# A chunked recurrence feeding a feed-forward layer on one Trainium2 core: the scores of unit 13 and two row splits are planned two steps later

## The chip, the cores and the metric

One NeuronCore of a Trainium2 chip runs the whole program. The metric is the device time of one execution in microseconds (us), median of the runs. The profile is one execution, taken by the hardware profiler. It shows five engines: PE (matmul; PEld is its weight load), DVE (VectorE), ACT (ScalarE), POOL (GpSimd) and SP, which here only issues DMAs. An engine works through its own instructions strictly in the order in which they stand in its program, and waits for semaphores of the others.

## The reference, cut to what is computed

A recurrence over 768 tokens per batch and head (4 batches, 8 heads, head size 32, state size 16), in chunks of 32 tokens, and then a feed-forward layer over all 3072 tokens (256 to 2048 to 256):

```
for c in range(S // 32):                       # chunk c of 32 tokens
    L = exp(cum_i - cum_j) * causal            # decays within the chunk
    y[c] = ((C @ B.T) * L) @ x + (C @ state) * exp(cum)
    state = decay_full * state + sum_j B_j x_j * decay_from_j
x = y as [3072, 256]
h = x @ w_in                                   # 256 -> 2048
g = softplus(h)
out = g @ w_out                                # 2048 -> 256
```

## The kernel before, in words

**Units and tiles.** The recurrence is cut into 24 units (`NB * NU`) of 128 tokens, six to a batch, with all heads in one unit. The feed-forward layer works on six tiles (`sizes`) of 512 tokens, so four units fill one tile: units 8 to 11 are the third tile (index 2), units 12 to 15 the fourth (index 3). The first 12 units are worked off in a hand-written order (`ORDER`, lines 59 to 76), and so is much of tiles 0 and 1. From unit 12 on (`FIRST`) the units are planned into steps (lines 919 to 926).

**Steps.** A step `s` stands for one tile and one block `k` of 128 of the 2048 hidden columns (line 896). Its first product, `hp`, is six matmuls of 512 columns on PE; then ACT makes `e` (softplus) and `gh` (the rounded high part), and DVE makes `gl` (the remainder). Four steps later (`LAG`) the second product takes `gh` and `gl` and adds six matmuls into two accumulators, `acc0` and `acc1`. There is one PSUM buffer for each of the two accumulators (pool `pa`, line 116). When a tile, or a half of the tiles 0 and 1, ends, DVE reads both out (`o0`, `o1`, line 803, which for tile 1 also adds the half kept in `half_1`) before PE may start the next tile's sums in them. Steps 0 to 31 are tiles 0 and 1, step 32 is the third tile's block 0, and its second product is therefore called at step 36. At such a step the next first product is put ahead of it (lines 937 and 938), so that two first products, twelve matmuls, stand on PE between the last sum of tile 1 and the first of the third tile.

**A unit's work, in the order in which it is planned.** `prefetch` loads the unit's rows (`un`, 256 KB), its spread B and C rows (`bc`, 512 KB) and, for each pair, the growth factors (`gg`). `split_whole` makes `c_all` (odd units) or `kc` (even units) from `bc` on ACT and DVE, has it copied by two DMAs into `c_rows`, of which there is a single buffer, and makes `b_rows`. `attend_scores` has POOL make the masked decays `rm`, PE the scores `sp` from `c_rows` and `b_rows`, and DVE the weighted scores `m`, then `bp` and `cc`. `pair_values` and `pair_ends` follow for a pair of units: `zp` and `yp` on PE, `state` and `tb` on DVE, then the output `y` and its parts `xh` and `xl`, which are the tile's input to the first products.

**What sets the order.** PE's instructions and SP's DMAs stay in the order in which the code calls them (lines 133 and 137 to 139). Up to step 30 (`PINNED`) the order on ACT, DVE and POOL is the code's as well; what is called from step 31 on is put in place there by the framework's scheduler, which may set it among the earlier, fixed instructions. All DMAs go through SP's queue: one that waits holds back all behind it.

**Names.** In profile rows buffer numbers are left out. In the order's rows `m13_1624` is the weighted scores of unit 13, `gl2_3` is block 3 of the third tile, `o0_1` is the half 0 of the output of tile 1, and the number at the end only tells buffers apart. A row of the order that has several equal instructions says so (x2).

Of the kernel before, what the change touches and what calls it, by code (L numbers as in the profile page):

```python
# [76 lines left out]
HALF = NFT // 2  # L77
AHEAD = 28
PINNED = 31
LAG = 4  # L80
# [26 lines left out]
def recurrence_then_ffn(ctx: ExitStack, tc: tile.TileContext, fst, un, alr, w_in, w_out, const, outT):  # L107
# [801 lines left out]
    def plan(s, f, *args):  # L909
        fills[s].append((f, args))  # L910

    def through(f):
        def run(*args):
            for _ in f(*args):
                pass

        return run

    for i in range(FIRST, NB * NU):
        s = 30 + 4 * (i - FIRST)  # L920
        plan(max(s - 4, AHEAD), split_whole, i)
        plan(s, attend_scores, i)
        plan(s + 1, prefetch, i + 3)
        if i % 2:
            plan(s + 2, through(pair_values), i - 1)
            plan(s + 3, through(pair_ends), i - 1)
# [73 lines left out]
```

## Time and profile before

| | us |
|---|---|
| median of 3 runs (325.82 to 326.68) | 326.49 |
| the profiled execution | 326.83 |
| its span, first to last instruction | 325.1 |
| PE busy (1974 instructions) | 318.3 (98%) |
| DVE busy | 190.6 (59% of the span) |
| ACT busy | 191.1 (59%) |
| POOL busy | 39.4 (12%) |

In the views below, times count from the span's start. A timeline row has the start, the duration, the engine, the line, the operation with its tiles, and in brackets how long the engine sat idle before it and which instruction released it. SPq rows are DMA issues: the time shown is what SP took to hand the transfer over, not the transfer. A matmul of 512 columns is shown with 0.39, but the next one starts about 0.23 after it; starts are what to compare. The line of most instructions is that of a helper (L129), so the tiles tell them apart. A row of the view by stretches has the stretch, then the busy time of PE, PEld, DVE, ACT and POOL with the instructions in brackets, the granted clock, the DMA engines' busy share and GB/s.

### The profile page before, as it was taken

How to read it: one execution, taken by the hardware profiler on the slowest of the kernel's cores; microseconds unless marked ns; L12 is line 12 of the kernel's file. 1: busy time of each engine (PE TensorE's matmuls, PEld its weight loads, DVE VectorE, ACT ScalarE, POOL GpSimd, SP SyncE). 2: the span in 40 equal slices, each digit the busy share in tenths (PEclk: the TensorE clock that was granted, in tenths of full speed). 3: DMA queues.
4: the chain of work that ended last, by engine and by line, in shares of the span. 5: the costliest groups of instructions: out<-in, count | busy, mean ns of one | idle time of the engine just before them, and what ended most of it. 6: DMA issues, size and time to landing. Idle time of an engine off the chain costs nothing.

```text
span 325.1 us, 5266 instructions
## 1 busy us (share of the span) xinstructions
PE 318.3 (98%) x1974; PEld 255.7 (79%) x1974; DVE 190.6 (59%) x338; ACT 191.1 (59%) x349; POOL 39.4 (12%) x42
## 2 busy tenths in 40 slices
PE   8999999999999999899999999999999999999996
PEld 3568888888878888588888888888888888888885
DVE  3799767889584566775646746675744433322222
ACT  4898989797877565544433824644633344544450
POOL 3545300210300001102202101012100000000000
PEclk9999999999999999999999999999999999999999
DMA  6949658661732154335125246125201000100001
GB/s 222 394 152 359 212 187 214 176 194 46 246 100 66 65 151 124 107 124 143 32 99 159 70 130 146 51 97 161 86 14 34 0 2 0 53 12 2 1 0 65
DMA packets 25178, 36.53 MB, mean 112 GB/s; under 512 B 2112, under 2 KB 13504, under 8 KB 25152
## 3 DMA queue, kind: packets, MB, share of 16 engines
q1 hardware_dynamic: 25152, 36.19, 36.0%
q8 instruction: 15, 0.25, 0.3%
q14 instruction: 11, 0.09, 0.1%
HBM read 28.74 MB, written 3.24 MB: 98 GB/s over the span
## 4 chain that ended last, share of the span: by engine, by line
PE 88%; DVE 4%; DMA 3%; SPq 2%; issue 2%; ACT 0%; POOL 0%; DVEq 0%; ACTq 0%; POOLq 0%
PE hp L129 38%; PE acc L129 37%; PE yp L129 6%; PE sp L129 4%; PE warm L129 2%; DMA un<-in_un 2%; SPq L139 2%; DMA bc<-in_un 1%; PE zp L129 1%; PE end L129 1%; DVE m L129 1%; DVE w L129 1%; PE gp L129 0%; DVE b_rows L292 0%; DVE o L803 0%
## 5 line engine op out<-in xcount | busy, mean ns | idle before, releaser
L732 DVE TENSOR_TENSOR gl<-e,gh 128x512 fp32r<-128x512 f32 x65 | 49.8, 771 | 50.0 <-ACT gh L726 48.9
L129 PE MATMUL hp<-xh,wih 128*128 128x512 f32 (+1 forms) x204 | 77.6, 380 | 0.0
L129 PE MATMUL hp<-xl,wih 128*128 128x512 f32 (+1 forms) x204 | 76.9, 377 | 0.0
L129 PE MATMUL hp<-xh,wil 128*128 128x512 f32 (+1 forms) x204 | 76.8, 377 | 0.0
L720 ACT ACTIVATE e<-hp 128x512 f32<-128x512 f32 x65 | 38.7, 595 | 64.6 <-PE hp L129 64.2
L129 PE MATMUL acc<-gh,woh 128*128 128x512 f32 x188 | 74.9, 399 | 1.5 <-DVE o L803 1.5
L129 PE MATMUL acc<-gh,wol 128*128 128x512 f32 x188 | 73.4, 390 | 0.1
L129 PE MATMUL acc<-gl,woh 128*128 128x512 f32 x188 | 73.5, 391 | 0.0
L129 PEld LDWEIGHTS hp<-xh,wih 128*128 128x128 f32 x204 | 38.4, 188 | 8.3 <-DVE xl L129 1.0
L726 ACT CAST gh<-e 128x512 fp32r<-128x512 f32 x65 | 40.2, 619 | 6.7 <-PE acc L129 4.0
L129 PEld LDWEIGHTS hp<-xh,wil 128*128 128x128 f32 x204 | 38.3, 188 | 7.1
L129 PEld LDWEIGHTS hp<-xl,wih 128*128 128x128 f32 x204 | 38.4, 188 | 6.9
L129 PEld LDWEIGHTS acc<-gh,woh 128*128 128x128 f32 x188 | 35.4, 188 | 9.0 <-DVE o L803 1.4
L129 PEld LDWEIGHTS acc<-gh,wol 128*128 128x128 f32 x188 | 35.3, 188 | 8.1 <-DVE wol L129 0.6
L129 PEld LDWEIGHTS acc<-gl,woh 128*128 128x128 f32 x188 | 35.4, 188 | 6.4 <-DVE gl L732 0.2
L402 POOL TENSOR_SCALAR_AFFINE_SELECT rm<-fc 128x1024 f32<-128x1024 f32 x11 | 16.8, 1531 | 129.8 <-DVE m L457 97.2
L129 DVE TENSOR_TENSOR gl<-e,gh 128x512 fp32r<-128x512 f32 x31 | 21.5, 701 | 9.6 <-ACT gh L129 9.5
L129 POOL TENSOR_SCALAR_AFFINE_SELECT rm<-fc 128x1024 f32<-128x1024 f32 x13 | 19.0, 1466 | 63.5 <-DVE m L129 58.4
L129 ACT ACTIVATE signs<-wraw 128x512 f16<-128x512 f32 (+1 forms) x32 | 24.1, 776 | 0.0
L129 ACT ACTIVATE e<-hp 128x512 f32<-128x512 f32 x31 | 18.2, 594 | 7.5 <-PE hp L129 7.2
L129 ACT CAST gh<-e 128x512 fp32r<-128x512 f32 x31 | 19.0, 617 | 3.5 <-PE acc L129 3.3
L129 DVE TENSOR_TENSOR m<-sp,rm 128x512 f32<-128x512 f32 x26 | 17.2, 681 | 1.0 <-PE sp L129 1.0
(103 smaller groups left out, 306.8 us busy)
## 6 DMA issues: line engine op xcount, KB each, us to landing
bc<-in_un SPq DMA_DIRECT2D x16, 512.0 KB
wraw<-in_w_in SPq DMA_DIRECT2D x8, 512.0 KB
wraw<-in_w_out SPq DMA_DIRECT2D x8, 512.0 KB
un<-in_un SPq DMA_DIRECT2D x16, 256.0 KB
out_t<-o SPq DMA_DIRECT2D x9, 256.0 KB
gg<-gd SPq DMA_DIRECT2D x16, 128.0 KB
c_rows<-c_all SPq DMA_DIRECT2D x16, 128.0 KB
c_rows<-kc SPq DMA_DIRECT2D x16, 128.0 KB
```

The costliest lines, as they stand in the source:

```text
L129: return lambda *a, **k: tc.keep_in_program_order(f(*a, **k))
L139: tc.keep_in_program_order(nc.sync.dma_start(out, in_))
L402: Pl.affine_select(out=rm.rearrange("p h c i -> p (h c) i"), in_=fc[:, u].rearrange("p h c -> p (h c)").unsqueeze(2).broadcast_to([P, NH * ...
L720: A.activation(e, h, AF.Softplus)
L726: A.copy(gh, e)
L732: V.tensor_tensor(gl, e, gh.bitcast(F32), op=ALU.subtract)
```

## The change

Two lines of the planning loop become five:

```
     for i in range(FIRST, NB * NU):
         s = 30 + 4 * (i - FIRST)
-        plan(max(s - 4, AHEAD), split_whole, i)
+        halt = 2 * HALF * 2 + LAG
+        if s < halt <= s + 2:
+            s += 2
+        plan(s - 2 if s - 4 == halt - 2 else max(s - 4, AHEAD), split_whole, i)
         plan(s, attend_scores, i)
         plan(s + 1, prefetch, i + 3)
         if i % 2:
             plan(s + 2, through(pair_values), i - 1)
             plan(s + 3, through(pair_ends), i - 1)
```

`halt` is 36, the step at which the third tile's second products begin. Only units 13 and 14 are touched. For unit 13, `s` goes from 34 to 36: its split from step 30 to 32, its scores from 34 to 36, the prefetch of unit 16 from 35 to 37, and the values and ends of the pair 12 and 13 from 36 and 37 to 38 and 39. For unit 14 only the split goes from 34 to 36. No instruction is added or removed on any engine: the counts are 339 on DVE, 328 on ACT, 45 on POOL and 105 rows on SP in both programs.

On PE, the four matmuls `sp13` stood between the third tile's first product 2 and tile 1's last sums; they now stand after the first sums of the third tile. The `zp` and `yp` matmuls of units 12 and 13 stood right after those first sums; they now stand after first product 6, and `sp14` right behind them.

DVE at the end of tile 1, before:

```order
L292 SCALAR_TENSOR_TENSOR c_all15_1790<-bc15_1560,kb_76,c_all15_1790 128x512
L457 TENSOR_TENSOR m13_1624<-sp13_0_1621,rm13_1619 128x512
L457 TENSOR_TENSOR m13_1624<-sp13_1_1626,rm13_1619 128x512
L803 TENSOR_TENSOR o0_1_1647<-acc0_1_1457,half_1_1223 128x512
L292 SCALAR_TENSOR_TENSOR b_rows15_1789<-bc15_1560,kb_76,b_rows15_1789 128x512
L803 TENSOR_TENSOR o1_1_1650<-acc1_1_1458,half_1_1223 128x512
```

and now:

```order
L732 TENSOR_TENSOR gl2_1_1598<-e2_1_1594,gh2_1_1596 128x512
L803 TENSOR_TENSOR o0_1_1625<-acc0_1_1457,half_1_1223 128x512
L803 TENSOR_TENSOR o1_1_1628<-acc1_1_1458,half_1_1223 128x512
L732 TENSOR_TENSOR gl2_2_1617<-e2_2_1613,gh2_2_1615 128x512
L732 TENSOR_TENSOR gl2_3_1642<-e2_3_1638,gh2_3_1640 128x512
L457 TENSOR_TENSOR m13_1670<-sp13_0_1667,rm13_1665 128x512
```

Before, the two read-outs `o0_1` and `o1_1` stand behind `c_all15` and both `m13`, with `b_rows15` between them. Now they stand next to each other, ahead of `m13`; `c_all15` stands just ahead of `gl2_0` and `gl2_1`, and `b_rows15` six rows behind `o1_1`.

DVE earlier in the program, where units 8 to 11 end and the weights of `w_out` are still being split (`wol1` is a part of these weights), before:

```order
L129 TENSOR_TENSOR y10_1294<-yp10_1238,gg10_1088 128x512
L129 TENSOR_TENSOR xl_2_1081<-y10_1294,xh_2_1080 128x2x256
L129 TENSOR_TENSOR wol1_1083<-w11_1200,woh1_1082 128x512
L129 TENSOR_TENSOR gl0_11_1316<-e0_11_1176,gh0_11_1195 128x512
L129 TENSOR_TENSOR gl0_12_1321<-e0_12_1283,gh0_12_1306 128x512
```

and now:

```order
L129 TENSOR_TENSOR y10_1294<-yp10_1238,gg10_1088 128x512
L292 SCALAR_TENSOR_TENSOR c_all13_1574<-bc13_1230,kb_76,c_all13_1574 128x512
L129 TENSOR_TENSOR xl_2_1081<-y10_1294,xh_2_1080 128x2x256
L129 TENSOR_TENSOR wol1_1083<-w11_1200,woh1_1082 128x512
L129 TENSOR_TENSOR gl0_11_1316<-e0_11_1176,gh0_11_1195 128x512
L129 TENSOR_TENSOR gl0_12_1321<-e0_12_1283,gh0_12_1306 128x512
```

The scheduler has set DVE's `c_all13` in there; before, it stood 30 rows further down, behind `bp14`. ACT's half of `c_all13` moves the same way: it now stands between `e0_12` and the cast `xh_2` of `y10`, and before it stood behind `gh1_14`.

SP's DMAs from unit 13's copies on, before:

```order
L139 DMA c_rows_88<-c_all13_1532 64x4x128 x2
L139 DMA un15_1558<-in_un 128x512
L139 DMA bc15_1560<-in_un 128x1024
L139 DMA c_rows_88<-kc_75 64x4x128 x2
L139 DMA out_t<-o0_1_1647 128x512
L139 DMA out_t<-o1_1_1650 128x512
L139 DMA un16_1666<-in_un 128x512
L139 DMA bc16_1668<-in_un 128x1024
```

and now:

```order
L139 DMA un15_1550<-in_un 128x512
L139 DMA bc15_1552<-in_un 128x1024
L139 DMA c_rows_88<-c_all13_1574 64x4x128 x2
L139 DMA out_t<-o0_1_1625 128x512
L139 DMA out_t<-o1_1_1628 128x512
L139 DMA c_rows_88<-kc_75 64x4x128 x2
L139 DMA un16_1706<-in_un 128x512
L139 DMA bc16_1708<-in_un 128x1024
L139 DMA gg16_1710<-gd_86 128x1x256 x2
```

The loads of unit 15 now stand ahead of the copies of `c_all13`, and the output of tile 1 ahead of the copies of `kc` for unit 14. The loads of unit 16 still follow, and `gg16` follows them in both.

More of the change, by code (lines that the diff above doesn't have):

```diff
@@ L920, in recurrence_then_ffn @@
         s = 30 + 4 * (i - FIRST)
-        plan(max(s - 4, AHEAD), split_whole, i)
+        halt = 2 * HALF * 2 + LAG
+        if s < halt <= s + 2:
+            s += 2
+        plan(s - 2 if s - 4 == halt - 2 else max(s - 4, AHEAD), split_whole, i)
         plan(s, attend_scores, i)
```

## The prediction

> **What bounds the kernel now.** I read the page's chain of work that ended last, then the list of PE's waits, then the timeline at the longest of them.
>
> ```profile
> PE 88%; DVE 4%; DMA 3%; SPq 2%; issue 2%; ACT 0%; POOL 0%; DVEq 0%; ACTq 0%; POOLq 0%
> PE acc L129 <- DVE o L803: 1.5, 2, 0.9
> PE warm L129 <- POOL some L129: 1.0, 1, 1.0
> ```
>
> PE holds 88% of the chain, so a stall of PE moves the end one for one, and work of other engines counts only where PE waits for it. The rows of the list have the waiting group, what it waited for, the total, the times and the longest. Its longest entry is the one this change is about: PE waits twice for `o`, the read-out of the accumulators (line 803). The next, `warm`, is the program's first work.
>
> In the timeline of PE at that wait, and in the chain's row for twelve matmuls elsewhere:
>
> ```profile
> 134.03 0.39 PE L129 MATMUL hp<-xh,wil 128*128 128x512 f32 x1
> 134.97 0.47 PE L129 MATMUL acc<-gh,woh 128*128 128x512 f32 x1 [0.55 <-DVE o L803]
> 135.51 0.40 PE L129 MATMUL acc<-gh,wol 128*128 128x512 f32 x1
> 136.82 0.50 PE L129 MATMUL acc<-gh,woh 128*128 128x512 f32 x1 [0.92 <-DVE o L803]
> 137.39 0.40 PE L129 MATMUL acc<-gh,wol 128*128 128x512 f32 x1
> 137.72 0.43 PE L129 MATMUL zp<-un,bp 128*32 128x64 f32 x16
> 282.42 2.72 PE hp L129 x12
> ```
>
> Twelve undisturbed matmuls take 2.72, so one follows another after 0.227. After the `hp` matmul at 134.03 the first sum was due at 134.26, and the sixth at 134.26 + 5 x 0.227 = 135.39. It started at 137.39. **The stop costs 2.00 us**: 0.71 at the first wait, 1.08 at the second, the rest slow starts behind them. The list has only 1.5, since it counts from the modelled ends.
>
> Why `o` is late, from ACT, DVE, POOL and SP just before:
>
> ```profile
> 127.22 0.45 SPq L139 DMA_DIRECT2D bc<-in_un  x1
> 131.52 0.72 ACT L290 ACTIVATE c_all<-bc,kb 128x512 fp32r<-128x512 f32 x1 [3.11 <-DMA bc<-in_un]
> 132.28 0.75 DVE L292 SCALAR_TENSOR_TENSOR c_all<-bc,kb,c_all 128x512 fp32r<-128x512 f32 x1 [1.86 <-ACT c_all L290]
> 132.94 1.28 DVE L457 TENSOR_TENSOR m<-sp,rm 128x512 f32<-128x512 f32 x2
> 134.14 0.68 DVE L803 TENSOR_TENSOR o<-acc,half 128x512 f32<-128x512 f32 x1
> 134.36 1.28 POOL L402 TENSOR_SCALAR_AFFINE_SELECT rm<-fc 128x1024 f32<-128x1024 f32 x1 [11.29 <-DVE m L457]
> 134.74 1.43 DVE L292 SCALAR_TENSOR_TENSOR b_rows<-bc,kb,b_rows 128x512 fp32r<-128x512 f32 x1
> 136.09 0.68 DVE L803 TENSOR_TENSOR o<-acc,half 128x512 f32<-128x512 f32 x1
> ```
>
> ACT waits 3.11 for unit 15's 512 KB (issued at 127.22) to make `c_all`; DVE stands behind it at `c_all`, idle for 1.86, then does both `m` of unit 13, and only then the first `o`, at 134.14. Then comes `b_rows`, 1.43 where its like, `c_all`, took 0.75, beside POOL's `rm`, which that same `m` released. The second `o` starts at 136.09.
>
> **The change part by part.** No instruction is added or removed, so the sum holds only stalls that go and stalls that come.
>
> *The stall that goes.* The `m` of unit 13 stand behind both `o` now, `b_rows15` too, and `c_all15` three rows ahead. What else holds the `o`?
>
> ```profile
> 129.67 0.64 PE L129 MATMUL sp<-c_rows,b_rows 128*128 128x256 f32 x4
> 130.15 0.40 PE L129 MATMUL acc<-gh,woh 128*128 128x512 f32 x1
> 110.09 1.28 DVE L129 TENSOR_TENSOR half<-acc,half 128x512 f32<-128x512 f32 x2
> 127.78 0.62 ACT L726 CAST gh<-e 128x512 fp32r<-128x512 f32 x1
> 117.51 1.18 SPq L139 DMA_DIRECT2D gg<-gd  x2
> ```
>
> Without `sp` at 129.67 (four matmuls, 0.48 until the next sum at 130.15) tile 1's last sums start there and take 1.36, until 131.0; two first products follow until 133.75. So the first `o` can start near 130.5, when its accumulator's three sums are over, and the second at 131.1, if DVE is free; a pair of such read-outs took 1.28 (110.09). Both are over by 132.5, **1.2 us before PE asks**. DVE is free earlier: the `gl` just ahead of the pair needs the `gh` of 127.78, hence ends near 129. And `c_all15` ahead of that needs unit 15's rows: they are asked for directly behind the `gg` of 117.51, so at about 119.4 instead of 127.22, and with the 4.3 that they took from issue to ACT (127.22 to 131.52) they are there at 123.7. What would be late next is `gl2_1`, and that has over a microsecond. Term: **-2.0**, bounds -2.1 and, should the old order of waits somehow come back, 0.
>
> *A new wait, at 94.* The scheduler moved `c_all13` from behind `bp14` to between `y10` and `xl_2`. Its input is unit 13's 512 KB, and behind it queue, on ACT the cast `xh_2` and what follows, and on DVE `xl_2` and then `wol1`, for which PE has a matmul:
>
> ```profile
> 89.89 0.34 SPq L139 DMA_DIRECT2D bc<-in_un  x1
> 92.66 0.61 ACT L129 ACTIVATE e<-hp 128x512 f32<-128x512 f32 x1
> 94.13 0.62 ACT L129 CAST xh<-y 128x512 fp32r<-128x512 f32 x1 [0.86 <-DVE y L129]
> 93.41 0.68 DVE L129 TENSOR_TENSOR y<-yp,gg 128x512 f32<-128x512 f32 x1
> 94.78 0.69 DVE L129 TENSOR_TENSOR xl<-y,xh 128x512 fp32r<-128x512 f32 x1 [0.69 <-ACT xh L129]
> 95.39 0.68 DVE L129 TENSOR_TENSOR wol<-w,woh 128x512 fp32r<-128x512 f32 x1
> 96.84 0.39 PE L129 MATMUL acc<-gh,wol 128*128 128x512 f32 x1
> 90.75:93.00 2.25, 2.17 (x12) 1.54 (x12) 1.67 (x5) 2.25 (x5) 0.00 (x0) 1.00 0.89 244
> 93.00:94.00 1.00, 1.00 (x6) 0.82 (x5) 1.00 (x2) 0.27 (x1) 0.00 (x0) 1.00 0.62 238
> ```
>
> The load is issued at 89.89 with unit 12's 256 KB right behind, and in the stretches (GB/s last) 549 kB have moved by 93.0 and 786 kB, both loads, by 94.0. So it lands between 93.0 and some 94.5; by 4.3 after its issue it would be 94.2. I take 93.8. Then ACT's half runs 93.8 to 94.5 (it is free from 93.27), DVE's half starts at 94.55 and hands on after 0.66 (132.28 to 132.94), so `xl_2` starts at 95.2 and not 94.78, and `wol1` ends at 96.5 and not 96.07. PE has that matmul at 96.84 and loads its weights one place, 0.23, earlier: 96.6. The delay of 0.4 just fits. At 94.2 `wol1` ends at 96.9, which costs 0.2; at 94.5, 0.5. Term: **+0.1**, bounds 0 and 0.5; past 93.9 it costs one for one. The Trainium skill (DMA: Bandwidth & Descriptors, "Queues, rings and completion order") says that each DMA engine takes one queue's descriptors in the order of its ring. By that, unit 13's bytes go before unit 12's, the early landing holds and the term is 0; the two stretches fit it without proving it.
>
> *What moves later: unit 16's loads, and what hangs on them.*
>
> ```profile
> 138.64 0.34 SPq L139 DMA_DIRECT2D un<-in_un  x1
> 139.04 0.42 SPq L139 DMA_DIRECT2D bc<-in_un  x1
> 142.70 0.73 ACT L290 ACTIVATE kc<-bc,kb 128x512 fp32r<-128x512 f32 x1
> 142.45 0.69 DVE L614 TENSOR_TENSOR y<-yp,gg 128x512 f32<-128x512 f32 x1 [0.81 <-PE yp L129]
> 143.17 1.17 SPq L139 DMA_DIRECT2D gg<-gd  x2
> 137.96 1.06 PE L129 MATMUL yp<-m,un 128*32 128x128 f32 x32
> 115.06 1.25 SPq L139 DMA_DIRECT2D c_rows<-kc  x2
> 118.20 0.71 PE L129 MATMUL sp<-c_rows,b_rows 128*128 128x256 f32 x4
> ```
>
> PE after the change: first sums of the third tile from 133.75, `sp13` from 135.1, four blocks of 1.36 until 141.0, `zp` and `yp` (1.3, from 137.72 to 139.0) until 142.4, `sp14` until 142.9, two blocks and `yp`'s last four matmuls, taken as 0.4 like the four of `sp`, until 146.0, six blocks until **154.2: `sp15`**. Before, unit 16's `un` (138.64) was issued 0.68 after `yp` began (137.96), which reads the buffer that it takes. Now `yp` begins at 141.3, so `un` goes out at 142.0 and `bc` at 142.4. Its landing took at most 3.66 (139.04 to 142.70): 146.1. ACT and DVE make `kc` (0.73 and 0.75): 147.6. Only behind that DVE has `y12`: 148.3. Then SP issues `gg16`, which takes the buffer `y12` has read (before: 142.45, 143.17), until 149.6, and then the copies for `sp15`. Such copies were there at most 3.14 after their issue (115.06 to 118.20): 152.7. **Cover: 1.5 us.** Term 0, bounds 0 and what a slower landing makes: with 4.3 for 3.66 it still fits. ACT is held at `kc` until 146.1, and DVE with it; the sums that need the `gh` and `gl` queued there, block 7's, stand behind `sp15`. Unit 14's copies wait now for `sp13` (135.6) and have, with 3.14, until 142.4: 3.6 of cover. Unit 13's copies go out at 120, for 135.1. POOL's `rm` follows `m13` to about 137, far from the `o`, and is next asked for at 154.6.
>
> *The moved matmuls themselves.* `sp13`, `zp`, `yp` are the same instructions between other neighbours. The slow starts shown above are 0.1 each, and one place more or less has them: +0.1, bounds -0.1 and 0.2.
>
> **Sum.** -2.0 + 0.1 + 0.1 = -1.8. Against the profiled execution, 326.83 with its span of 325.1 and 1.7 around it, that gives 325.0; this execution was 0.34 above the median of the three runs, so off the median, 326.49, it is **324.7**.
>
> **The rivals.** *The load at 94 is late:* it lands at 94.5, the sums wait 0.5, 325.1. For it speaks that the margin is 0.1, against it that the bytes of this load alone are covered by 93.0.
>
> *The read-outs stay late:* DVE is held at `c_all15`, now ahead of `gl2_0`, until after 133. It would take a landing 9 us later than worked out. That is the case in which the change doesn't do what it says: 326.5.
>
> *`sp15` waits in part:* the chain from `yp` to the copies is one of six hand-overs, and every one took its shortest path in my sum. Late by 3.0, it costs 1.5: 326.2.
>
> *Slower:* the same chain, at the same place, late by more than 4.3: 1.5 are covered, 1.8 are the gain, and 1.0 is the 0.3% (of 326.49) that a measurement of this kernel can tell from no change. So it decides when unit 15's copies land after 157.0 where I have 152.7; late by 4.5 it gives 327.7. Against it speaks that no landing in the rows above took over 4.3, so that one would have to double.
>
> **How the numbers follow.** Forecast 0.72; the load at 94 late 0.10; read-outs still late 0.07; `sp15` in part 0.06; slower 0.05. Faster by over 0.3% means under 325.5: the first two, 0.82. Within: 0.13. Slower: 0.05. The range: down to 324.0 (bounds -2.1, 0 and -0.1, and 0.3 for runs that lie as far below their median as these), up to 325.9, which takes in the first rival and the milder part of the third, with the same allowance.
>
> **What would show it.** Right, if in the profile after, PE's waits have no `acc` behind `o`, the two `o` stand next to each other near 131, and the third tile's first sums follow twelve `hp` matmuls without a gap. ACT's `c_all` near 93.8, and PE's matmul of 96.84 within 0.2 of that, shows the second term; a wait of PE's weight load for `wol` there shows it mis-sized. `sp` near 154 without a wait shows the third. A gap of PE at any of these three, or one between 141 and 147, where four pieces of unit work now stand closer together, would make the prediction wrong.

## The result, and the profile after

The changed kernel took **330.0 us** (median of 4 runs, 327.84 to 330.31) against 326.15 for the kernel before beside it: a ratio of 1.0105, 95% interval 1.0057 to 1.0152. It is slower, where 324.7 was predicted. The profiled execution took 330.13 (span 328.4), that of the kernel before 326.83.

PE's list of waits in the changed kernel (group, what it waited for, total, times, longest):

```profile
PE sp L129 <- DMA c_rows<-c_all: 2.7, 1, 2.7
PE warm L129 <- POOL some L129: 1.0, 1, 1.0
PE yp L129 <- ACT e L129: 0.6, 1, 0.6
PE sp L129 <- DVE m L129: 0.6, 1, 0.6
```

The wait for `o` is gone. A new one is longer: `sp15` waits for the copies of `c_all15`. The two small ones of 0.6 lie in the program's first 36 us; two later profiles of the same kernel have at most 0.3 there. In this one PE's matmuls from 36 to 128 stand 0.88 later than in the kernel before. That much of this execution is its start, and it is taken off below wherever a time is compared with the prediction ("less 0.88").

The place of the old wait, in the timeline of the changed kernel and in its chain of waits (start, length, engine, group):

```profile
132.68 1.28 DVE L803 TENSOR_TENSOR o<-acc,half 128x512 f32<-128x512 f32 x2
132.07 2.72 PE hp L129 x12
134.79 1.36 PE acc L129 x6
```

Both read-outs run without a gap and end at 133.96; PE does the twelve matmuls of two first products in 2.72 and goes straight on to the third tile's sums. The new wait, from SP, ACT, DVE and PE:

```profile
143.38 0.38 SPq L139 DMA_DIRECT2D bc<-in_un  x1
148.54 0.72 ACT L290 ACTIVATE kc<-bc,kb 128x512 fp32r<-128x512 f32 x1 [5.16 <-DMA bc<-in_un]
149.29 0.75 DVE L292 SCALAR_TENSOR_TENSOR kc<-bc,kb,kc 128x512 fp32r<-128x512 f32 x1 [2.12 <-ACT kc L290]
149.96 0.68 DVE L614 TENSOR_TENSOR y<-yp,gg 128x512 f32<-128x512 f32 x1
150.67 1.19 SPq L139 DMA_DIRECT2D gg<-gd  x2
151.97 1.37 SPq L139 DMA_DIRECT2D c_rows<-c_all  x2
158.11 1.19 PE L129 MATMUL sp<-c_rows,b_rows 128*128 128x256 f32 x4 [2.75 <-DMA c_rows<-c_all]
```

This is the chain that the prediction's third part walks through, link by link; it was to be done 1.5 us early and is 2.75 late. And PE doesn't come back at full speed, as the view by stretches shows (PE, PEld, DVE, ACT, POOL busy, granted clock, DMA share, GB/s):

```profile
158.00:159.00 1.00, 0.89 (x4) 0.92 (x5) 0.01 (x1) 0.00 (x0) 0.00 (x0) 0.50 0.23 90
159.00:160.00 1.00, 1.00 (x5) 0.81 (x5) 0.68 (x1) 0.23 (x1) 0.00 (x0) 0.50 0.01 4
160.00:161.00 1.00, 1.00 (x4) 0.81 (x3) 0.47 (x1) 1.00 (x3) 0.00 (x0) 0.50 0.34 80
161.00:162.00 1.00, 1.00 (x6) 0.77 (x5) 1.00 (x3) 1.00 (x2) 0.00 (x0) 0.86 0.79 180
159.31 2.35 PE acc L129 x6
```

The granted clock is 0.50 for some 3.4 us. The six sums behind `sp15` take 2.35 in place of the 1.36 above. The balance of the two profiled executions: 2.0 gained at the read-outs (by the prediction's count), 2.9 lost in the wait (`sp15` was due at 155.20, when the last matmul ahead of it had run, and started at 158.11), 1.5 at half clock, 0.9 at the start, hence +3.3, from 326.83 to 330.13. Of the four runs the three near 330 have a mean granted clock of 0.995 or less, the one at 327.84 has 1.000.

### The profile page after: what moved, and what is told of

Its sections match the earlier page's. It is cut to its first block, busy times and chain, and to the rows that moved or that the text cites. A ratio compares the mean times of both kernels' runs of the same rounds, so it can differ in the third digit from the quotient of the medians.

```text
span 328.4 us, 5260 instructions
## 1 busy us (share of the span) xinstructions
PE 319.0 (97%) x1974; PEld 256.8 (78%) x1974; DVE 191.5 (58%) x338; ACT 191.2 (58%) x349; POOL 38.8 (12%) x42
## 4 chain that ended last, share of the span: by engine, by line
PE 82%; DMA 9%; SPq 3%; ACT 2%; DVE 1%; issue 1%; ACTq 0%
PE acc L129 36%; PE hp L129 35%; PE yp L129 5%; PE sp L129 4%; SPq L139 3%; DMA head_in_l<-in_fst 2%; DMA un<-in_fst 2%; DMA un<-in_un 2%; DMA c_rows<-c_all 2%; DMA bc<-in_un 2%; PE end L129 1%; PE zp L129 1%; ACT e L129 0%; PE fp L129 0%; ACT cc L129 0%
## 5 line engine op out<-in xcount | busy, mean ns | idle before, releaser
L457 DVE TENSOR_TENSOR m<-sp,rm 128x512 f32<-128x512 f32 x22 | 14.2, 684 | 8.4 <-PE sp L129 8.4
```

What stands on the lines that cost most here:

```text
L457: V.tensor_tensor(mid[i]["m"][:, 4 * g : 4 * g + 4].rearrange("p h t -> p (h t)"), mid[i].pop(("sp", g)), mid[i]["rm"][:, 4 * g : 4 * g + ...
```

## The experiments

All times are medians; ratios are against the kernel before, run beside them on the same chip (326.2, 326.5, 326.2 and 326.2 in the four series). "Issue" is when SP begins to issue the copies of `c_all15`. The trace has sixteen completion marks for each such copy, spread over time; "landed" is the last mark of the second copy.

| run | sp15 waits | issue | landed, after | us | ratio (95%) |
|---|---|---|---|---|---|
| changed again | 2.74 | 150.62 | 156.71, 6.1 | 327.95 | 1.0047 (1.0029 to 1.0066) |
| gg16 behind the copies | none | 144.71 | 150.97, 6.3 | **324.89** | 0.9960 (0.9943 to 0.9976) |
| y12 ahead of kc16 | 0.15 | 148.47 | 154.61, 6.1 | 326.29 | 0.9999 (0.9981 to 1.0017) |
| wait filled | 0.2 | 151.45 | 157.63, 6.2 | 327.84 | 1.0047 (1.0031 to 1.0062) |
| before, gg16 behind the copies | none | 146.58 | 149.72, 3.1 | 326.42 | 1.0000 (0.9981 to 1.0019) |
| pair one step earlier | 0.3 | 147.02 | 153.52, 6.5 | 325.10 | 0.9967 (0.9950 to 0.9984) |
| one head of gg16 ahead | none | 150.05 | 153.18, 3.1 | 324.89 | 0.9961 (0.9940 to 0.9983) |
| half of gg16 ahead | 1.03 | 149.70 | 154.79, 5.1 | 325.86 | 0.9990 (0.9973 to 1.0008) |
| changed, third series | 2.55 | 151.51 | 157.51, 6.0 | 329.18 | 1.0098 (1.0070 to 1.0126) |
| unit 17's loads ahead | 4.73 | 151.81 | 159.16, 7.4 | 332.45 | 1.0190 (1.0162 to 1.0218) |
| wait filled, third series | none | 151.00 | 157.14, 6.1 | 328.18 | 1.0060 (1.0037 to 1.0083) |
| gg16 in eight transfers | 2.15 | 153.47 | 156.57, 3.1 | 328.38 | 1.0068 (1.0046 to 1.0089) |

**The changed kernel again.**

> The changed kernel itself, for its spread. Its profile has sp15 waiting 2.75 us for the copies of c_all15, and the next sums at 0.63 us for a matmul instead of 0.39. Theory: wait and slow clock come together, so a run either has both (about 330) or little of both (about 328, as one of four had). Rival: the spread comes from the start of the program, before 36 us, where the profiled run is 0.9 us late; then the wait at sp15 is the same in every run and the times spread evenly.

```profile
156.84 0.71 PE L129 MATMUL sp<-c_rows,b_rows 128*128 128x256 f32 x4 [2.74 <-DMA c_rows<-c_all]
157.00:158.00 1.00, 1.00 (x7) 0.91 (x7) 0.58 (x1) 0.00 (x0) 0.00 (x0) 1.00 0.10 41
```

The timeline row and the stretch behind it: the same wait, but here the clock stays at 1.00, in all six runs, and the time is 327.95. The wait was there in all three profiles of this kernel; the half clock comes and goes.

**gg16 behind the copies.** `gg16` waits for `y12` and holds up SP; now unit 15's copies and unit 17's loads go first.

```
-            if i % 2 == 0:
+            if i % 2 == 0 and i != 16:
                 load_growth(i)
...
     plan(AHEAD, prefetch, FIRST + 2)
+    plan(40, load_growth, 16)
```

> Unit 16's growth factors (gg16) are asked for at step 40, behind the copies of c_all15 and the loads of unit 17, not ahead of them; nothing else is moved. Theory (the copies for sp15 are late because SP has to wait with gg16 for y12, and y12 for unit 16's rows): the copies go out when sp14 is done, near 144, land by 150, sp15 at about 155 waits for nothing, no slow matmuls, and the gain at the read-outs stands alone: 324.3 to 325.2. Rival (the removed stall at the read-outs was never on the path, something else in the second half took its place): 326 to 330 and PE waits elsewhere.

SP's rows, and the longest of PE's waits, in this run:

```profile
144.07 0.38 SPq L139 DMA_DIRECT2D bc<-in_un  x1
144.71 1.25 SPq L139 DMA_DIRECT2D c_rows<-c_all  x2
151.99 1.18 SPq L139 DMA_DIRECT2D gg<-gd  x2
PE warm L129 <- POOL some L129: 1.0, 1, 1.0
```

The copies go out right behind unit 16's loads, `sp15` doesn't wait, and the change is then a gain: 0.2 to 0.6% below the kernel before, within 0.2 us of the predicted time. So the wait of the third part, with the clock that follows it, is what separates the result from the forecast, and a version faster than both kernels is found. The copies took 6.3 here too, but in another way: of each copy's sixteen marks fifteen came within 4.2 of its issue and only the last after 5.6 to 5.8. Unit 16's load just ahead has one such late mark as well; the last section takes it up.

**y12 ahead of kc16.** DVE made `kc16` first, after waiting for unit 16's rows, and `y12`, which releases `gg16`, only then. Here the split of unit 16 keeps its place in the code, behind `y12`.

```
     def split_whole(i):
+        held, in_order[0] = in_order[0], in_order[0] or i == 16
...
+        in_order[0] = held
```

> The split of unit 16 keeps its place in program order on ACT and DVE, so y12 no longer stands behind kc16, which waits for unit 16's 512 KB; SP's order stays as in the changed kernel. Theory (the hold of DVE at kc16 is the root): y12 comes about 3 us earlier, near 147, gg16 at 148, the copies at 149.4; with the 6 us they took behind gg16 they land at 155.4 for a sp15 due at 155.2: a wait of 0 to 0.5, 324.5 to 325.5. Rival (the slow landing of the copies behind gg16 is the main part, and the issue time matters little): a wait of 1.5 or more, 327 to 329.

SP's issue of `gg16`, then the place of a new wait on PE, with ACT and DVE just before it:

```profile
147.18 1.18 SPq L139 DMA_DIRECT2D gg<-gd  x2
180.09 0.72 ACT L290 ACTIVATE c_all<-bc,kb 128x512 fp32r<-128x512 f32 x1 [5.79 <-DMA bc<-in_un]
183.74 1.28 DVE L459 TENSOR_TENSOR m<-sp,rm 128x512 f32<-128x512 f32 x2
184.94 0.68 DVE L807 COPY o<-acc 128x512 f32<-128x512 f32 x1
185.76 0.47 PE L129 MATMUL acc<-gh,woh 128*128 128x512 f32 x1 [1.04 <-ACT e L722]
```

`gg16` goes out 2.2 us earlier and the wait at `sp15` falls to 0.15: the hold by `kc16` is real. But the fixed order moves the later work too: DVE makes its half of `kc16` only at 159.68 (147.95 in the changed kernel run again), and SP issues unit 18's `bc` at 164.62, no earlier than there (164.26), though PE is 2.1 ahead at `sp15`. And a tile further on PE stops for 1.04 at the same kind of place as in the kernel before: a split waits for its load, and `m` and then the read-out `o` stand behind it. (The view names ACT's `e`, which ended at about the same moment; the sums need the accumulator that `o` reads until 185.62.) Net against the changed kernel: 1.7 us of the 2.6.

**The wait filled.** Twelve matmuls whose result nothing uses stand ahead of `sp15`.

```
+        if i == 15 and g == 0:
+            xh = x_parts(starts[2])[0][0]
+            for k in range(12):
+                PE.matmul(sp, wih[:, k % 2, :P], xh[:, k % 2, :], start=True, stop=True)
```

> Twelve matmuls of 512 columns are added on PE right ahead of sp15, into the buffer that sp15's first matmuls then overwrite; they keep PE busy for 2.7 us of the wait. Theory (of the loss at sp15, about 1.5 us is the halved clock after the idle time): sp15 starts when it did, its matmuls and the next sums run at full speed, 328.2 to 329.0. Rival (the slow matmuls come from the late input or cost nothing in the end): 330 as before, or more where the copies are not late and the twelve are pure cost (328 plus 2.7).

327.84, equal to the changed kernel beside it. The twelve run from 154.64 to 157.52 in a wait that ends at 157.77, so they cost nothing; but on this chip the changed kernel showed no half clock either, so nothing follows for the clock yet. The same pair is run again below.

**The kernel before, with gg16 behind the copies.** The edit that puts `gg16` behind the copies, made in the kernel before.

> The kernel before, with nothing changed but the place of unit 16's growth factors gg16: in SP's queue they stand behind unit 15's copies and unit 17's loads, not ahead of them. In the kernel before, sp15 never waited, so if the gain of the run with gg16 behind the copies came from taking away the wait that the change had brought, this move is worth nothing here: 326.2 us, within 0.3% of the kernel before, and PE still waits 1.5 to 2 us for the read-outs o. Rival: gg16 ahead of the copies costs something by itself in either kernel (SP held for y12); then this run is faster too, by 0.5 us or more.

Ratio 1.0000: no gain, as the theory said. With no `gg16` and no other load right ahead of them in the queue the copies land 3.1 after their issue. The profile has the old wait, smaller:

```profile
PE acc L129 <- DVE o L803: 0.9, 1, 0.9
135.44 0.39 PE L129 MATMUL hp<-xh,wil 128*128 128x512 f32 x1
138.30 0.40 PE L129 MATMUL acc<-gh,wol 128*128 128x512 f32 x1
135.05 0.68 DVE L803 TENSOR_TENSOR o<-acc,half 128x512 f32<-128x512 f32 x1
137.00 0.68 DVE L803 TENSOR_TENSOR o<-acc,half 128x512 f32<-128x512 f32 x1
```

By the prediction's own count (the sixth sum due 6 x 0.227 after the last `hp` at 135.44, so at 136.80; it started at 138.30) the stall costs 1.50 in this execution, not 2.00.

**The pair one step earlier.** Scores of unit 13 as changed; the values and ends of the pair 12 and 13, from which unit 16's loads hang, at steps 37 and 38.

```
+        if i == 13:
+            s -= 1
         if i % 2:
             plan(s + 2, through(pair_values), i - 1)
```

> The changed kernel, with the values and ends of the pair 12 and 13 planned one step (about 2.7 us) earlier, at steps 37 and 38; everything else as changed, gg16 again ahead of the copies. By the theory that the chain yp, unit 16's loads, kc16, y12, gg16, copies is what makes sp15 late, each link comes about 2.7 us earlier, so the 2.74 us that sp15 waited is all but gone (0 to 0.5) and the time is 327.95 - 2.7 = 325.2 (324.7 to 325.8). If it is instead the later place of unit 13's scores itself that costs, the time stays near 328. Rival in between: the pair's matmuls now stand one block behind sp13 and wait for its weighted scores m13; then yp waits there and gives part back, 326 to 327.

```profile
141.59 0.38 SPq L139 DMA_DIRECT2D bc<-in_un  x1
145.72 1.18 SPq L139 DMA_DIRECT2D gg<-gd  x2
147.02 1.36 SPq L139 DMA_DIRECT2D c_rows<-c_all  x2
PE sp L129 <- DMA c_rows<-c_all: 0.3, 1, 0.3
```

325.1, as expected. The copies go out at 147.02 and `sp15` waits 0.3, although they still take 6.5. It was the late pair that made the change slower, not the late scores.

**One head of gg16 ahead, and half of it.** Are gg16's bytes what makes the copies take 6 us, or only that SP is held until `y12`? Here 32 KB of it, or 128 KB, stay ahead (SP is held as before), and the rest goes behind unit 17's loads.

```
+    later = []
...
+            if i == 16 and g == 0:
+                load(gg[:D, 0, :], gd[b, 0, at].unsqueeze(0).broadcast_to([D, n * P]))
+                later.append(lambda: load(gg[D:, 0, :], gd[b, 1:4, at].unsqueeze(1).broadcast_to([3, D, n * P])))
+                continue
...
+    plan(40, lambda: [f() for f in later])
```

> The changed kernel, where only one head's part of gg16 (32 KB of 256 KB) stands ahead of unit 15's copies in SP's queue, so that SP is still held until y12 is made, and the rest of gg16 follows behind unit 17's loads. Theory: gg16's bytes are what the copies wait for, because its transfers move at about 96 GB/s, a quarter of the DMA engines, and the copies stand behind them on those. Then the copies, issued near 150, land some 3.5 us after their issue instead of 6.0, sp15 waits 0 to 0.3 us, and the time is about 325.3. Rival: the copies take 6 us because unit 17's 768 KB follow right behind them, or because that is what they take here; then they land near 156, sp15 waits about 2 us, and the time is about 327.

> The changed kernel, where one of gg16's two transfers (128 KB) stands ahead of unit 15's copies and the other behind unit 17's loads: half the dose. By the theory of gg16's bytes (96 GB/s, so 128 KB take 1.35 us) the copies are issued near 150.0 and land 6.0 - 1.35 = 4.7 us later, near 154.7, sp15 waits 0.5 to 0.9 us, time about 325.9. By the rival (6 us whatever stands ahead) they land near 156, sp15 waits about 2 us, time about 327.

One head, then half, each from SP's rows and PE's `sp15`:

```profile
149.63 0.33 SPq L139 DMA_DIRECT2D gg<-gd  x1
150.05 1.28 SPq L139 DMA_DIRECT2D c_rows<-c_all  x2
153.98 0.64 PE L129 MATMUL sp<-c_rows,b_rows 128*128 128x256 f32 x4
```

```profile
149.03 0.57 SPq L139 DMA_DIRECT2D gg<-gd  x1
149.70 1.30 SPq L139 DMA_DIRECT2D c_rows<-c_all  x2
154.92 0.71 PE L129 MATMUL sp<-c_rows,b_rows 128*128 128x256 f32 x4 [1.03 <-DMA c_rows<-c_all]
```

With 32 KB ahead the copies land 3.1 us after their issue, with 128 KB 5.1, with 256 KB 6.1; unit 17's loads follow in all three, so they aren't the cause. SP is free of `y12` at about the same time in all three as well: the 3 us are gg16's. The half costs more than its share (4.7 expected), but a single head also differs in kind: it is another form of transfer. The last run takes that up.

**The clock: the changed kernel a third time, more ahead of the copies, and the wait filled.** For the second of these, unit 17's loads are called one step earlier, ahead of the copies:

```
-        plan(s + 1, prefetch, i + 3)
+        plan(s + 1 if i != 14 else s, prefetch, i + 3)
```

> The changed kernel once more, beside the next two. Theory: sp15 always waits 2.7 us, and whether PE's granted clock halves for some 3.5 us after it (1.5 us lost) differs between executions. Then executions with a mean clock of 1.000 lie near 328.0 and those at 0.995 or less near 330. If the clock has nothing to do with it, times and mean clock show no such pairing.

> The changed kernel, with unit 17's loads (768 KB) called one step earlier, so that they too stand ahead of unit 15's copies: more bytes ahead of them. Theory of the bytes ahead: the copies are issued 1.4 us later, the loads take 2.2 us more at the 350 GB/s that the loads of unit 16 show, sp15 waits 4 to 5 us instead of 2.7. With so long an idle time the theory of the clock expects half clock after it in every execution: 328.0 + 1.3 to 2.3 + 1.5 = 330.8 to 331.8, mean clock 0.995 or less. Without a drop of the clock: 329.3 to 330.3 at 1.000. If the copies take 6 us whatever stands ahead, sp15 waits 4.1 by the later issue alone.

> The changed kernel with 12 matmuls of 512 columns ahead of sp15, whose result nothing uses (sp15 overwrites it); they lie in PE's wait, so that it isn't idle. Theory of the clock: no execution shows a clock under 0.998, all lie near 328, also where the changed kernel beside it shows executions of 330. If executions near 330 come here too, idle time of PE isn't what sets them.

| | runs at a mean clock of 1.000 | runs at 0.995 or less |
|---|---|---|
| changed, third series | 327.46, 328.18, 329.18 | 328.91, 330.21, 330.30, 330.36 |
| unit 17's loads ahead (wait 4.7) | none | 331.45, 332.34, 332.57, 332.70 |
| wait filled | 327.42 to 328.88, all six | none |

A stretch behind `sp15` with the loads ahead, and the filling matmuls in the third run:

```profile
160.00:161.00 1.00, 1.00 (x5) 0.81 (x4) 0.97 (x2) 1.00 (x3) 0.00 (x0) 0.50 0.00 0
154.38 2.88 PE L129 MATMUL sp<-xh,wih 128*128 128x512 f32 x12
```

After 4.7 idle every execution runs at half clock; after 2.6 some do; with the idle time filled none does, on a chip where the unfilled kernel beside it does in four of seven. So the idle time of PE is what trips it, as far as six executions against seven can show. The pairing of clock and time is not perfect (329.18 at 1.000, 328.91 at 0.995). The loads ahead also add to the copies, which land 7.4 after their issue (1.3 more, where 2.2 were expected), and `sp15` waits the 4 to 5 that were expected; the time, 332.45, is 0.6 above the range given for it.

**gg16 in eight transfers.** The same 256 KB ahead, one head each.

```
-            if i < EARLY:
+            if i < EARLY or i == 16:
                 for h in range(4):
                     load(gg[h * D : h * D + D, g, :], gd[b, g * 4 + h, at].unsqueeze(0).broadcast_to([D, n * P]))
...
             load(gg[:, g, :], gd[b, g * 4 : g * 4 + 4, at].unsqueeze(1).broadcast_to([4, D, n * P]))
```

> The changed kernel, with gg16 loaded by eight transfers of one head each (32 partitions, 32 KB) in place of two of four heads: the same 256 KB stand ahead of unit 15's copies. SP takes about 0.42 each, so the copies are issued 2.1 us later after gg16's first issue than in the changed kernel (3.4 instead of 1.3). Theory of the few engines: what holds the copies is that a transfer of four heads moves at about 96 GB/s, a quarter of the DMA engines, and the copies' parts on these engines come last; the single head ahead in an earlier run was spread over all. Then the copies land 3.1 to 3.6 us after their issue in place of 6.1, sp15 waits 1.6 to 2.2 us, about 327.2 where PE's clock stays full. Rival: the 256 KB ahead count, however they are spread: then 6 us again, sp15 waits 4.5 us or more, 330 or more.

```profile
149.79 3.58 SPq L139 DMA_DIRECT2D gg<-gd  x8
153.47 1.26 SPq L139 DMA_DIRECT2D c_rows<-c_all  x2
156.66 0.71 PE L129 MATMUL sp<-c_rows,b_rows 128*128 128x256 f32 x4 [2.15 <-DMA c_rows<-c_all]
```

The copies land 3.1 after their issue with all 256 KB ahead, as without them; the longer issue (3.58 in place of 1.19) gives 2.4 back. By itself this run doesn't part the form of gg16's transfers from the delay: the copies go out 3.7 after gg16's first issue in place of 1.3, and by then five of the eight had landed. In the kernel before, with the old form and 2.5 between the two issues, the same copies took 4.7; on the trend from 6.1 to 4.7, 3.7 between them would give about 3.3 (an estimate from these two rows).

The completion marks part them. Times are from each transfer's own issue:

| run | the two copies' sixteen marks each |
|---|---|
| the changed kernel | twelve at 2.4 to 2.7, four at 4.7 to 5.3 |
| half of gg16 ahead | twelve at 2.6 to 3.0, four at 4.2 to 4.4 |
| one head ahead | all at 2.2 to 2.5 |
| gg16 in eight transfers | all at 2.2 to 2.5 |

In the changed kernel each of gg16's own two transfers has, besides one mark at 1.0, only four, at 3.3 to 3.7 and 4.8 to 5.2, where a transfer of one head has sixteen close together, at 1.4 to 2.0. This fits a gg16 that sits on four of the sixteen DMA engines (their busy share, in the last section, says the same): the copies' parts on these four come after it, and the other twelve parts aren't held. So the form of gg16's transfers, which puts all their bytes on four engines, makes the copies late. The median of 328.38 mixes five executions at full clock (mean 327.5) and five at 0.995 (mean 328.9), after a wait of 2.15.

## Why the prediction was wrong, by its own steps

**What bounds the kernel** held: PE's matmuls behind the wait stand 3.31 later than in the kernel before, and the end comes 3.30 later; in the changed kernel run again it is 0.56 and 0.57.

**The stall that goes** (-2.0): right in mechanism; there is no wait for `o` in any run with the change. The size was that of one execution: another shows 1.50, and the three versions without the new wait gain 1.3 (gg16 behind the copies), 1.4 (pair earlier) and 1.6 (one head ahead). The cover was taken as 1.2 for the pair; by the same count it is 0.7, from 133.96 to the first sum at 134.63. Half a microsecond of it went by the same mistake as in the third part, a landing behind a `gg` priced from a place without one; that no wait came of it is luck:

```profile
120.65 1.34 SPq L139 DMA_DIRECT2D c_rows<-c_all  x2
129.02 0.72 ACT L290 ACTIVATE c_all<-bc,kb 128x512 fp32r<-128x512 f32 x1 [3.79 <-DMA c_rows<-c_all]
```

`c_all15` was to have its rows at 123.7. They were asked for at 120.18, shortly behind a `gg` (118.39), and their last mark is at 128.17, 8.0 later where 4.3 was taken. And `c_all` has a single buffer (line 295), which the sum left out: the copies of `c_all13` read it, and they landed at 129.00, 8.35 after their issue. So ACT's `c_all` ran at 128.1 (129.02 less 0.88), and the pair of read-outs began at 131.8 in place of 130.5.

**The wait at 94** (+0.1): zero. ACT's `c_all` ran at 94.60, which less the late start of 0.88 is 93.7 (93.8 predicted), and PE didn't wait.

**Unit 16's loads and what hangs on them** (0, "cover 1.5 us"): this is the step that failed. The order of its links was right, and so were the ends: `bc` issued at 143.38, less 0.88 is 142.5 (predicted 142.4); `sp15` due at 155.2, less 0.88 is 154.3 (predicted 154.2). Two landings between them were not:

- Unit 16's rows: 3.66 taken, 5.16 measured (143.38 to 148.54). This made `kc16`, `y12`, `gg16` and the copies' issue 1.5 late each (151.97 less 0.88 is 151.1; predicted 149.6). Why these rows were late is read from the traces in the last section and not tested.
- The copies: 3.14 taken, from a place where no gg stood right ahead of them; 6.0 measured. Another 2.9.

Together 4.4, of which 1.5 were covered: 2.9 of wait, where the profile has 2.75. That is the fourth rival, "late by more than 4.3", at its own price: 327.7 predicted for it, 327.95 measured where the clock stays full. It got too small a chance from a bad argument: "no landing in the rows above took over 4.3". Those rows are all landings that someone waited for, or bounds by what ran next. The kernel before had copies behind a `gg` in the queue:

```profile
145.65 1.31 SPq L139 DMA_DIRECT2D c_rows<-c_all  x2
170.47 1.18 SPq L139 DMA_DIRECT2D gg<-gd  x2
171.76 1.37 SPq L139 DMA_DIRECT2D c_rows<-c_all  x2
```

The first row is the very copies of `c_all15`, issued 2.5 behind gg16's 143.17: their landing mark is at 150.37, 4.7 later, already over 4.3. The last stands right behind a `gg`, as in the change: landed at 177.93, 6.2 later. Nobody waited for either, so no view of waits lists them.

**Not in the sum at all:** what an idle PE costs afterwards. Five executions at either clock in the last run lie 1.5 us apart, and that is what separates 328 from 330.

**The moved matmuls** (+0.1, held): 20.45 predicted without it from the third tile's first sum to `sp15`'s due time, 20.57 measured (134.63 to 155.20).

## What to carry to other kernels

When a load is moved, price each landing behind it from a place with the same neighbours in the queue, not from the nearest landing of the same size; a landing that nobody waited for has a completion mark in the trace and is as good a row. A chain of six hand-overs that each take their shortest time has no cover until its slowest links are bounded too. And a wait of a few microseconds on PE can cost more than its length: here the clock dropped behind it in some executions, for another 1.5.

## What the runs showed of the hardware

**A broadcast load on a quarter of the engines.** With gg16 alone on the queue (gg16 behind the copies), a stretch shows:

```profile
155.00:156.00 1.00, 1.00 (x7) 0.84 (x5) 0.54 (x2) 0.73 (x2) 0.00 (x0) 1.00 0.27 96
```

The DMA engines are busy for 0.27 and move 96 GB/s; the changed kernel's load of unit 16 has all of them:

```profile
145.00:146.00 1.00, 1.00 (x6) 0.84 (x5) 0.86 (x3) 0.00 (x0) 0.24 (x1) 1.00 0.99 375
```

The Trainium skill (DMA: Bandwidth & Descriptors, "Rules for kernel authors") says that an outermost dimension of a size below 16 confines a whole DMA to at most so many engines. `gg` has four heads there, and the trace agrees: 0.27 of 16 engines is about four, and each of its transfers has four late completion marks. The copies' parts on these four come last, as the marks of the last run's section show.

**A load that meets an instruction fetch.** The DMA view of the changed kernel from 142 to 149 has, in 40 equal slices, GB/s with a tail, and one packet of another queue:

```profile
GB/s 0 0 0 0 0 0 0 0 0 0 0 152 117 105 269 374 468 328 456 351 328 421 421 351 187 94 23 0 23 23 23 23 23 23 0 0 0 0 0 0
q8 instruction: 1, 0.02, 0.9%
```

From 146.6 to 148 the last packets of unit 16 trickle in at 23 GB/s, a sixteenth of the 375 above, so from one engine: of the 512 KB load's sixteen completion marks fifteen come within 3.6 of its issue, which is what the prediction took, and the last after 5.05. The trace has the instruction packet (16 KB) at 145.32 for 0.98, inside the load. In ten profiles in which that packet fell inside this load, its last byte came 4.2 to 4.8 after its issue; in the three in which it didn't (the kernel before, the same with gg16 behind the copies, the pair one step earlier), 3.2 to 3.8; the changed kernel with gg16 behind the copies, where fifteen marks came within 4.1 and the last after 5.7, is left out, since the copies share the engines with the load there. No run moved the fetch by itself, so this is read from the traces and not tested.

**Half clock after less than 3 us of idle time.** It is read off the mean granted clock of each execution, and the length of the idle time off the one that was profiled. It came in three of four executions, none of six, and four of seven after 2.55 to 2.75, in five of ten after 2.15, in four of four after 4.7, and in none of sixteen with the time filled. The Trainium skill (TensorE: Matmul & The Clock Gate, "HAM oscillation — how this bites in real kernels") gives the rule "no PE-idle gaps >~3.4µs". The runs here differ: the one profiled at half clock after less than 3.4 had 2.75, and with a profiled gap of 2.15 half of the executions show it, so the limit to plan with is lower. How low was not measured; with 1.03 (half of gg16 ahead) none of ten shows it.
